# A transposition of attention weights issued one step later in a two-feed-forward kernel

## The chip, the cores and the metric

The kernel runs on one core of a Trainium2 chip. The metric is the device time of one execution in microseconds (us), the median of several runs. A core has five engines that this text speaks of: TensorE (PE, matrix products; PEld is its loading of weights), VectorE (DVE), ScalarE (ACT), GpSimd (POOL) and SyncE (SP, which here issues the DMA transfers). Each works through its own queue in order; they wait for each other by semaphores. Products go to a memory of their own, PSUM, from which VectorE and ScalarE read them.

## The reference

12480 tokens of 128 features go through an attention over 32 inducing rows and back, then through two feed-forward layers of width 2048.

```python
def mab(q, kv):
    s = scale * (q @ kv.transpose(0, 2, 1))
    s = s - s.max(-1, keepdims=True)
    a = np.exp(s)
    a /= a.sum(-1, keepdims=True) + 1e-09
    return a @ kv
h = mab(I, x)                 # 32 inducing rows over all tokens
x = mab(x, h)                 # all tokens over the 32 rows
h = x @ w_in                  # first feed-forward
x = (h * np.clip(h + 3.0, 0.0, 6.0) / 6.0) @ w_out
r = np.maximum(x @ w2_in, 0.0)   # second feed-forward
return (r * r) @ w2_out
```

## The kernel before

The first pass (up to some 40 us) makes the 32 rows `h`. The second pass takes the tokens in 26 chunks of 480 (`CH`), each of four blocks of 120 (`BLK`). All is kept with the features on the partitions and the tokens along the row.

A chunk takes NP = 8 steps, numbered p = 0 to 7; k counts the steps of all chunks, c the chunks. In a step the kernel does two of the sixteen slices of 128 of both feed-forwards, the second one OFF = 11 steps behind the first, so with tokens of an earlier chunk. In each step of the repeating part TensorE runs, in this order:

- `up1`: two products into `h1` (line 567), from the chunk's attention weights `at`. The matrix product of attention with `h` and the first w_in are folded into one 128-row matrix `m4`; so `at` of a chunk is needed from its first step on.
- `up2`: six products into `h2` (line 643), from the first feed-forward's output in an upper and a lower part, `yh` and `yl`.
- in some steps, a part of the next chunk's attention.
- `down1` and `down2`: six products each into the accumulators `yacc` and `oacc` (line 614; in the first steps in plain float32, line 602), from steps L1 = 2 and L2 = 3 back.

That makes 20 products of 480 columns a step. Between them ScalarE and VectorE gate `h1` (`gate1`: a ReLU on ScalarE, line 574, then a product on VectorE, line 575), split the result into an upper part (`hi`, GpSimd, line 586) and a lower part (`lo`, VectorE, line 594), and do likewise for `h2` on ScalarE (lines 653, 657, 667) and VectorE (`lo`, line 673).

The next chunk's attention is spread over the steps of the current chunk: the scores at p = 1 (`att_scores`, tile `ps`), maximum and exponential at p = 2 (`att_exp`, tile `pst`), the norm at p = 4 (`att_norm`: on VectorE a sum, a reciprocal, a product, a cast and two subtractions, the last on line 540; on ScalarE a cast, line 538; the result is `a4`, shown as `a` in a profile), and the turn (`att_turn`). The turn lays the weights of 480 tokens, which lie with the tokens on the partitions, the other way round: four products with a unit matrix into the PSUM tile `pt` (line 550), and a copy on ScalarE from `pt` into `at` (line 555).

`h1`, `h2`, `ps`, `pst` and `pt` take turns in three PSUM buffers (`hp`, tag "h"): each new tile waits until the tile three before it has been read. The accumulators have buffers of their own.

What sets the order: in the first pass, and from step KM = 24 on (at 145 us or so), the order of the engines' queues is that of the code. For the steps before KM, in which the feed-forwards' weights, which come as float64, are also converted (lines 174 to 242, by a plan of ticks, on VectorE, ScalarE and GpSimd), a scheduler sets the order from the code's order and its own estimates. SyncE's order is the code's throughout.

Of the kernel before, what the change touches and what calls it, by code (L numbers as in the profile page):

```python
# [18 lines left out]
SP = mybir.EngineType.SP  # L19

P = 128
BLK = 120          # tokens of a block: one partition each
CH = 480           # tokens of a chunk: four blocks
EPS = 1e-09
CW = 512           # columns of a weight that are converted at a time

# groups of the first pass: tokens of the blocks of each of the four token runs
GROUPS = [(128,) * 2] + [(128,) * 4] * 4 + [(128, 128, 48), (128,) * 2, (128,) * 2]
KEPT = 5           # the group of the last tokens: it stays on chip for the first chunks
TURN_V = {}       # quarters of a group's turned blocks that VectorE copies, ScalarE the others  # L30
NATURAL = {7}      # groups that are loaded in both layouts
# loads of the first pass: groups of tokens (x, and n in the other layout), quarters of the first
# feed-forward's w_in (a) and w_out (b)
LOADS = [("x", 0), ("x", 1), ("x", 2), ("a", 0), ("x", 3), ("x", 4), ("a", 1), ("a", 3), ("a", 2),
         ("x", 5), ("b", 3), ("x", 6), ("b", 0), ("x", 7), ("n", 7), ("b", 2), ("b", 1)]
# for each quarter of the weights (a, b, and c, d for the second feed-forward): the ticks at which its
# conversion starts and at which it is cut in two (two ticks a group of the first pass, PRE up to the
# second pass, then two a step), the engines of the steps (v, p, s: VectorE, GpSimd, ScalarE), and
# whether the sign takes a product of its own
PLAN = {  # L40
    ("a", 0): (4, None, "--v", False),
    ("a", 1): (6, None, "--v", False),
# [12 lines left out]
    ("d", 2): (53, 62, "ssvpv", False),  # L55
    ("d", 3): (58, 62, "--vpv", False),
}
# steps whose parts go to another engine than the rest's
HIGH1_S = {0, 1, 3, 4, 6, 7, 9, 13, 14, 18, 19, 20, 22, 23}   # ScalarE instead of GpSimd
LOW1_P = {1, 2, 4, 5, 6, 7, 8, 11}    # GpSimd instead of VectorE  # L60
HIGH2_P = {0, 1, 6, 7, 10, 12}        # GpSimd instead of ScalarE
LOW2_P = {}  # GpSimd instead of VectorE
N1 = 13            # steps of the first w_out that go in float32 as it is
OFF = 11           # steps from a first product of one feed-forward to the other's
L1, L2 = 2, 3      # steps from a first product to the second
MIX = (0, 3)       # steps of the third and fourth quarter of the mixed weights
PRE = 26           # ticks before the second pass
KM = 24            # steps up to which the engines' order is the scheduler's
RA, RB = 4, 4      # quarters of the first w_in, of the other weights that are on chip as float64
WB = 8             # quarters that are there in float32  # L70
TAIL = 8           # last steps whose upper parts GpSimd makes
LAST = 2           # chunks that stay on chip from the first pass


@with_exitstack
def induced_attention_then_two_ffn(
# [44 lines left out]
    ep = ctx.enter_context(tc.tile_pool(name="ep", bufs=3))  # L121
    sp = ctx.enter_context(tc.tile_pool(name="sp", bufs=2))

    # the last groups of the first pass are the first chunks of the second: they are still on chip
    order = list(range(NCH - LAST, NCH)) + list(range(NCH - LAST))
    x_of = {}

# [3 lines left out]
        nc.sync.dma_start(t, xT[:, n:n + CH])  # L131
        x_of[c] = t

    # A float64 weight comes as two words. Its absolute value is rounded to float32 as
    # (2^20 + v) * power of two, v being the fraction's upper 20 bits with the lower word behind
    # the point; the sign is put on last. What is far below float32's range of use (2^-106) becomes
    # zero. Where an upper and a lower part are asked for, the two add up to the float32 exactly.
    engine_of = {"v": nc.vector, "p": nc.gpsimd, "s": nc.scalar}
    src_of = {"a": w1a, "b": w1b, "c": w2a, "d": w2b}

# [17 lines left out]

    whole, parts, raws, held = {}, {}, {}, []

    # the first feed-forward's w_in in float32 lies where the upper parts of its w_out come to lie
    def float_of(item):
        kind, q = item
        if kind == "a":
# [85 lines left out]
    live, ticks = [], []  # L250
# [22 lines left out]

    waiting = [(kind, q) for kind in "bcd" for q in range(4) if (kind, q) not in LOADS]

# [1 line left out]
    NKEEP = run[KEPT] * J  # L277
    assert LAST * CH <= NKEEP
    t0 = [sum(run[i] for i in range(g) if i != KEPT) * J for g in range(NG)]
# [3 lines left out]
    first = ExitStack()  # L283
    first.enter_context(tc.manual_schedule())
    with ExitStack() as pro:
        pp = pro.enter_context(tc.tile_pool(name="pp", bufs=1))
        pps = pro.enter_context(tc.tile_pool(name="pps", bufs=1, space=PSUM))

        # the tensor engine's clock comes up before the first tokens are there
        fill(18, pps, "xt", 4)  # L290

        nc.sync.dma_start(ind, indT)
# [94 lines left out]
                    )  # L387
            nc.scalar.copy(hsb[:, g, :], acc)

        # the groups' softmaxes brought to their common maximum  # L390
        def common_max():
            nmin = pp.tile([P, 1], F32, name="nmin")
            nc.vector.tensor_reduce(out=nmin, in_=nmax, axis=AX.X, op=ALU.min)
# [45 lines left out]
        rw, rl = weigh(nm4)  # L439
        accumulate(NG - 1)  # L440
        tick()
        # all groups but the last by their weights, four times below each other, and together
        pg = pps.tile([P, D], F32, tag="xt", name="pg", bufs=4)
        for g in range(NG - 1):
            j = g % J
# [20 lines left out]
        )  # L466
        tick()

# [1 line left out]
    hp = ctx.enter_context(tc.tile_pool(name="hp", bufs=3, space=PSUM))  # L470
    ap_ = ctx.enter_context(tc.tile_pool(name="accp", bufs=1, space=PSUM))
    wpool2 = ctx.enter_context(tc.tile_pool(name="wpool2", bufs=1))
# [3 lines left out]
        o = order[c] * CH - (NT - NKEEP)  # L476
        x_of[c] = xlast[:, o:o + CH]

    # inducing rows times w_in: the first feed-forward's weights on 32 rows, four times below
    # each other, as upper, upper, lower and lower parts  # L480
    mixed = {}

    def mix(q):
# [15 lines left out]
    def att_scores(c):  # L499
        ps = hp.tile([P, BLK], F32, tag="h", name="ps")  # L500
        for b in range(J):
            nc.tensor.matmul(  # L502
                ps[M * b:M * (b + 1), :], lhsT=ht4[:, 0, :], rhs=x_of[c][:, b * BLK:(b + 1) * BLK],
                start=True, stop=True,
            )
        s = sp.tile([P, BLK], F32, tag="s", name="s")
        nc.scalar.mul(s, ps, SCALE)
        att[c] = s

    def att_exp(c):  # L510
        s = att.pop(c)
        pt = hp.tile([BLK, J, M], F32, tag="h", name="pst")
        nc.tensor.transpose(pt.rearrange("p j i -> p (j i)"), s, ident)
# [128 lines left out]
            for n, (w, y) in enumerate(((wh, yh[c]), (wl, yh[c]), (wh, yl[c]))):  # L642
                nc.tensor.matmul(h2[k][:, u, :CH], lhsT=w, rhs=y, start=(n == 0), stop=(n == 2))  # L643

    # the last step goes in halves
    def sides(k):
        return (slice(0, 1), slice(1, 2)) if k == K - 1 else (slice(0, 2),)

# [68 lines left out]
    behind = ExitStack()  # L717
# [5 lines left out]
    for k in range(K + OFF + L2 + 1):  # L723
        if k == KM:
            behind.close()
            ctx.enter_context(tc.manual_schedule())
        c, p = divmod(k, NP)
        j = k - OFF
        on(up1, k)
        on(low1, k - 1)  # L730
        tick()
        on(gate1, k)
        on(high1, k)
        on(square2, j - 1)
        on(up2, j)
        on(relu2, j)
        on(high2, j - 1)
        on(low2, j - 2)
        tick()
        if k in MIX:  # L740
            q = MIX.index(k) + 2
            mix(q)
            mix_high(q)
            mix_low(q)
        if c + 1 < NCH:
            if p == 0 and LAST < c + 2 < NCH:
                load_x(c + 2)
            if p == 1:
                att_scores(c + 1)
            if p == 2:  # L750
                att_exp(c + 1)
            if p == 4:
                att_norm(c + 1)
            if p == 5:
                att_turn(c + 1)
        on(down1, k - L1)
        on(down2, j - L2)
# [28 lines left out]
```

## Time and profile before

| | us |
|---|---|
| median of 3 runs | 1013.14 |
| lowest and highest run | 1013.09, 1014.53 |
| span of the profiled execution | 1011.0 |
| TensorE busy | 985.3 |
| ScalarE busy | 845.3 |
| VectorE busy | 833.5 |
| GpSimd busy | 389.6 |

The span runs from the first to the last instruction of one profiled execution; it is 2.1 us below the median of the timed runs, which hold what lies around it as well. The page's parts are: the busy time of the engines, the chain of work that ended last (followed back from the last instruction to what released each), and the costliest groups. Apart from the page, a trace can be asked for waits (who waited for whom, in total, and how often) and for the timeline of an engine: start, duration, instruction and, in brackets, how long the engine was idle before it and what ended that. The durations of neighbouring products overlap, as they are pipelined; the distance between their starts is what a product costs in a row of them.

### The profile page before, as it was taken

To read this page: it belongs to the slowest core of one execution; us is meant where nothing else is said; L and a number is where in the kernel's file an instruction comes from. 1 tells how busy PE (TensorE), PEld (TensorE's weight loads), DVE (VectorE), ACT (ScalarE), POOL (GpSimd) and SP (SyncE) were. 2 spreads that over 40 slices of the span, in tenths; PEclk is the share of its full clock that TensorE was granted. 3 is DMA by queue.
4 is the path that set the end of the run, shared out by engine and by line. 5 is a ranking of instruction groups with operands and counts; after the bars stand their busy time and mean duration, and the time that the engine had idled before them with its cause. 6 is when DMAs were issued, how large, how long until landed. Compare 5 with 4: busy or idle time off the path is not lost.

```text
span 1011.0 us, 12988 instructions
## 1 busy us (share of the span) xinstructions
PE 985.3 (97%) x4911; PEld 818.1 (81%) x4911; DVE 833.5 (82%) x1012; ACT 845.3 (84%) x1041; POOL 389.6 (39%) x236
## 2 busy tenths in 40 slices
PE   9769999999999999999999999999999999999998
PEld 6436788888888888888888888888888888888887
DVE  5998978888888878888888887888888888788764
ACT  6657888888888888888888888888888888888886
POOL 0374433433334344343333434434333343443423
PEclk9899999999999999999999999999999999999999
DMA  9530000000000000000000000000000000000000
GB/s 343 172 113 10 1 20 20 1 20 21 1 20 20 20 1 20 21 1 20 20 1 20 20 20 1 20 20 0 20 20 1 20 20 19 2 11 10 1 10 20
DMA packets 15118, 28.44 MB, mean 28 GB/s; under 512 B 1360, under 2 KB 13008, under 8 KB 14544
## 3 DMA queue, kind: packets, MB, share of 16 engines
q1 hardware_dynamic: 15056, 27.61, 8.3%
q8 instruction: 39, 0.64, 0.3%
q14 instruction: 23, 0.19, 0.1%
HBM read 21.22 MB, written 6.39 MB: 27 GB/s over the span
## 4 chain that ended last, share of the span: by engine, by line
PE 79%; DVE 15%; ACT 2%; issue 1%; POOL 1%; DMA 1%; SPq 0%; ACTq 0%; POOLq 0%
PE oacc L614 23%; PE yacc L614 22%; PE h L643 21%; PE h L567 7%; DVE g L575 4%; DVE lo L673 2%; ACT g L574 1%; DVE lo L594 1%; PE pt L550 1%; POOL hi L586 1%; DVE le L529 1%; DVE a L540 1%; PE ps L502 1%; DMA raw<-in_w1a 1%; DVE cva L179 1%
## 5 line engine op out<-in xcount | busy, mean ns | idle before, releaser
L586 POOL TENSOR_SCALAR hi<-g 128x960 fp32r<-128x960 f32 x188 | 331.6, 1764 | 527.3 <-DVE g L575 527.3
L594 DVE TENSOR_TENSOR lo<-g,hi 128x960 fp32r<-128x960 f32 x195 | 226.9, 1163 | 95.7 <-POOL hi L586 93.2
L574 ACT ACTIVATE g<-h,three 128x960 f32<-128x960 f32 x208 | 220.7, 1062 | 91.8 <-PE h L567 91.7
L673 DVE TENSOR_TENSOR lo<-g,hi 128x960 fp32r<-128x960 f32 (+1 forms) x209 | 240.3, 1150 | 11.8 <-POOL hi L662 7.1
L575 DVE SCALAR_TENSOR_TENSOR g<-g,h 128x960 f32<-128x960 f32 x208 | 239.0, 1150 | 11.0 <-ACT g L574 7.7
L657 ACT ACTIVATE g<-g 128x960 f32<-128x960 f32 (+1 forms) x209 | 207.4, 993 | 0.3
L653 ACT ACTIVATE g<-h 128x960 f32<-128x960 f32 (+1 forms) x209 | 200.4, 960 | 6.1 <-PE h L643 6.1
L667 ACT CAST hi<-g 128x960 fp32r<-128x960 f32 x196 | 193.5, 988 | 0.0
L643 PE MATMUL h<-yh,wh 128*128 128x480 f32 x416 | 158.1, 380 | 0.0
L643 PE MATMUL h<-yh,wl 128*128 128x480 f32 x416 | 157.4, 378 | 0.0
L643 PE MATMUL h<-yl,wh 128*128 128x480 f32 x416 | 157.1, 378 | 0.0
L567 PE MATMUL h<-at,m 128*128 128x480 f32 x416 | 128.3, 390 | 0.6 <-ACT at L555 0.6
L614 PE MATMUL oacc<-hi,wh 128*128 128x480 f32 x416 | 124.9, 381 | 0.0
L614 PE MATMUL oacc<-lo,wh 128*128 128x480 f32 x416 | 124.1, 379 | 0.0
L614 PE MATMUL oacc<-hi,wl 128*128 128x480 f32 x416 | 123.2, 377 | 0.0
L614 PE MATMUL yacc<-hi,wh 128*128 128x480 f32 x390 | 121.6, 392 | 1.4 <-DVE yl L632 1.4
L614 PE MATMUL yacc<-hi,wl 128*128 128x480 f32 x390 | 115.9, 378 | 0.0
L614 PE MATMUL yacc<-lo,wh 128*128 128x480 f32 x390 | 115.9, 378 | 0.0
L567 PEld LDWEIGHTS h<-at,m 128*128 128x128 f32 x416 | 78.4, 190 | 18.3 <-issue 4.0
L643 PEld LDWEIGHTS h<-yh,wh 128*128 128x128 f32 x416 | 78.0, 188 | 13.1 <-ACT g L653 0.4
L614 PEld LDWEIGHTS oacc<-hi,wl 128*128 128x128 f32 x416 | 78.2, 188 | 12.5
L614 PEld LDWEIGHTS oacc<-hi,wh 128*128 128x128 f32 x416 | 77.9, 187 | 12.6 <-issue 0.4
(118 smaller groups left out, 947.1 us busy)
## 6 DMA issues: line engine op xcount, KB each, us to landing
outT<-osb SPq DMA_DIRECT2D x25, 240.0 KB, 2.0
xc<-in_xT SPq DMA_DIRECT2D x24, 240.0 KB, 2.6
xg<-in_xT SPq DMA_DIRECT2D x4, 1024.0 KB, 7.4
raw<-in_w1a SPq DMA_DIRECT2D x4, 512.0 KB, 8.8
raw<-in_w1b SPq DMA_DIRECT2D x4, 512.0 KB, 9.1
raw<-in_w2a SPq DMA_DIRECT2D x4, 512.0 KB, 3.8
raw<-in_w2b SPq DMA_DIRECT2D x4, 512.0 KB, 3.8
xg<-in_xT SPq DMA_DIRECT2D x3, 512.0 KB, 10.2
```

The source lines that it names most:

```text
L179: nc.vector.tensor_scalar(out=a, in0=high, scalar1=0xFFFFF, scalar2=0x100000, op0=ALU.bitwise_and, op1=ALU.bitwise_or,)
L567: nc.tensor.matmul(h1[k][:, u, :CH], lhsT=m4[:, f * P:(f + 1) * P], rhs=a_t[c], start=True, stop=True)
L574: nc.scalar.activation(g1[k], h, AF.Relu, bias=three)
L575: nc.vector.scalar_tensor_tensor(out=g1[k], in0=g1[k], scalar=6.0, in1=h, op0=ALU.min, op1=ALU.mult)
L586: nc.gpsimd.tensor_scalar(out=hi1[k], in0=g1[k], scalar1=1.0, scalar2=1.0, op0=ALU.mult, op1=ALU.mult)
L594: (nc.gpsimd if k in LOW1_P else nc.vector).tensor_tensor(out=lo1[k], in0=g1.pop(k), in1=hi1[k], op=ALU.subtract)
L614: nc.tensor.matmul(acc, lhsT=w[:, f * P:(f + 1) * P], rhs=g[:, u, :], start=(p == 0 and n == 0), stop=(p == NP - 1 and n == 5),)
L643: nc.tensor.matmul(h2[k][:, u, :CH], lhsT=w, rhs=y, start=(n == 0), stop=(n == 2))
L653: nc.scalar.activation(g2[k][:, u, :], h[:, u, :CH], AF.Relu)
L657: nc.scalar.activation(g2[k][:, u, :], g2[k][:, u, :], AF.Square)
L667: nc.scalar.copy(hi2[k][:, u, :], g2[k][:, u, :])
L673: (nc.gpsimd if k in LOW2_P else nc.vector).tensor_tensor(out=lo2[k][:, u, :], in0=g[:, u, :], in1=hi2[k][:, u, :], op=ALU.subtract)
```

## The change

`att_turn` of the next chunk is called at the end of the step p = 6 in place of p = 5. All else in the diff takes away comments and spaces.

```diff
             if p == 4:
                 att_norm(c + 1)
-            if p == 5:
+            if p == 6:
                 att_turn(c + 1)
         on(down1, k - L1)
```

In the built program this moves rows on TensorE and ScalarE in each chunk from KM on. TensorE in the middle of the run, before: the turn (`pt`) stands between `up2` of p = 5 (`h_3061`) and the `down` products of that step; `h_3096` is `up1` of p = 6.

```order
L643 MATMUL h_3061<-yl,wh 128x480
L550 MATMUL pt<-ident_r,a_3033 128x120 x4
L614 MATMUL yacc<-hi_2973,wh 128x480 x2
L614 MATMUL yacc<-hi_2973,wl 128x480 x2
L614 MATMUL yacc<-lo_3023,wh 128x480 x2
```

TensorE at the same place after; `h_3089` and `h_3100` are `up1` and `up2` of p = 6, and `hi_3009` belongs to `down1` of that step.

```order
L567 MATMUL h_3089<-at,m_78 128x480 x2
L643 MATMUL h_3100<-yh,wh 128x480
L643 MATMUL h_3100<-yh,wl 128x480
L643 MATMUL h_3100<-yl,wh 128x480
L643 MATMUL h_3100<-yh,wh 128x480
L643 MATMUL h_3100<-yh,wl 128x480
L643 MATMUL h_3100<-yl,wh 128x480
L550 MATMUL pt<-ident_r,a_3033 128x120 x4
L614 MATMUL yacc<-hi_3009,wh 128x480 x2
```

The turn now stands one whole step of TensorE later. ScalarE around the same turn, as a difference (`h_3096` of before is `h_3089` of after, and so on):

```order
 L667 CAST hi_3070<-g_3019 128x960
-L555 CAST at<-pt 128x480
-L574 ACTIVATE g_3101<-h_3096,three 128x960
+L574 ACTIVATE g_3094<-h_3089,three 128x960
 L657 ACTIVATE g_3068<-g_3068 128x960
-L653 ACTIVATE g_3114<-h_3107 128x960
-L667 CAST hi_3116<-g_3068 128x960
+L653 ACTIVATE g_3107<-h_3100 128x960
+L667 CAST hi_3109<-g_3068 128x960
+L555 CAST at<-pt 128x480
 L574 ACTIVATE g_3138<-h_3133,three 128x960
```

The copy out of `pt` has gone behind four instructions of the step p = 6. In the steps before KM the scheduler orders anew. VectorE there, in the first chunk of the second pass, before, from the conversions ahead of three gates (line 575) to the first `yl`:

```order
L205 TENSOR_SCALAR w_868<-raw 128x512
L189 SCALAR_TENSOR_TENSOR cva<-raw,cva 128x512
L174 TENSOR_SCALAR cve<-raw 128x512
L179 TENSOR_SCALAR cva<-raw 128x512
L240 CAST wh<-w_709 128x512
L575 SCALAR_TENSOR_TENSOR g_861<-g_861,h_852 128x960
L575 SCALAR_TENSOR_TENSOR g_876<-g_876,h_872 128x960
L575 SCALAR_TENSOR_TENSOR g_887<-g_887,h_884 128x960
L189 SCALAR_TENSOR_TENSOR cva<-raw,cva 128x512
L205 TENSOR_SCALAR w_982<-raw 128x512
L174 TENSOR_SCALAR cve<-raw 128x512
L575 SCALAR_TENSOR_TENSOR g_897<-g_897,h_894 128x960
```

VectorE at the same place after (`g_854` is `g_861` of before):

```order
L575 SCALAR_TENSOR_TENSOR g_854<-g_854,h_845 128x960
L189 SCALAR_TENSOR_TENSOR cva<-raw,cva 128x512
L205 TENSOR_SCALAR w_861<-raw 128x512
L575 SCALAR_TENSOR_TENSOR g_876<-g_876,h_872 128x960
L575 SCALAR_TENSOR_TENSOR g_887<-g_887,h_884 128x960
L174 TENSOR_SCALAR cve<-raw 128x512
L179 TENSOR_SCALAR cva<-raw 128x512
L575 SCALAR_TENSOR_TENSOR g_897<-g_897,h_894 128x960
L632 SCALAR_TENSOR_TENSOR yl<-yacc,yh 128x480
L515 TENSOR_REDUCE nm<-pst 120x4
L240 CAST wh<-w_709 128x512
```

The gates have moved ahead of conversions, and the cast `wh<-w_709` and a set of conversions (`w_982`) behind `yl`.

## Rows read from the trace of the kernel before

**Rows 1.** The page, parts 1 and 4: busy time, and the chain's shares.
```profile
PE 985.3 (97%) x4911; PEld 818.1 (81%) x4911; DVE 833.5 (82%) x1012; ACT 845.3 (84%) x1041; POOL 389.6 (39%) x236
...
PE 79%; DVE 15%; ACT 2%; issue 1%; POOL 1%; DMA 1%; SPq 0%; ACTq 0%; POOLq 0%
```

**Rows 2.** Waits from 140 us on: waiter, awaited, us, times, longest.
```profile
PEld pt L550 <- ACT a L538: 12.2, 22, 1.0
```

**Rows 3.** TensorE's timeline, mid run: start, duration, instruction, count, idle before.
```profile
597.90 0.59 PE L567 MATMUL h<-at,m 128*128 128x480 f32 x2
...
599.40 0.38 PE L643 MATMUL h<-yl,wh 128*128 128x480 f32 x1
599.93 0.63 PE L550 MATMUL pt<-ident_r,a 120*128 120x120 f32 x4
...
603.07 0.60 PE L567 MATMUL h<-at,m 128*128 128x480 f32 x2
...
607.39 0.59 PE L567 MATMUL h<-at,m 128*128 128x480 f32 x2
```

**Rows 4.** TensorE's timeline: an unwaited turn's step, then the first and last waiting ones.
```profile
127.71 0.59 PE L567 MATMUL h<-at,m 128*128 128x480 f32 x2
...
129.21 0.38 PE L643 MATMUL h<-yl,wh 128*128 128x480 f32 x1
129.43 0.55 PE L550 MATMUL pt<-ident_r,a 120*128 120x120 f32 x4
...
132.46 0.59 PE L567 MATMUL h<-at,m 128*128 128x480 f32 x2
...
163.84 0.59 PE L567 MATMUL h<-at,m 128*128 128x480 f32 x2
...
169.50 0.59 PE L567 MATMUL h<-at,m 128*128 128x480 f32 x2
...
923.03 0.59 PE L567 MATMUL h<-at,m 128*128 128x480 f32 x2
...
928.23 0.59 PE L567 MATMUL h<-at,m 128*128 128x480 f32 x2
```

**Rows 5.** VectorE's timeline, mid run, around the turn of rows 3.
```profile
599.29 0.49 DVE L540 TENSOR_TENSOR a<-a,a 120x128 fp32r<-120x128 f32 x2
...
600.77 1.15 DVE L575 SCALAR_TENSOR_TENSOR g<-g,h 128x960 f32<-128x960 f32 x1
...
603.27 0.66 DVE L686 COPY osb<-oacc 128x480 f32<-128x480 f32 x1 [0.28 <-PE oacc L614]
...
604.96 1.15 DVE L575 SCALAR_TENSOR_TENSOR g<-g,h 128x960 f32<-128x960 f32 x1
```

**Rows 6.** ScalarE's timeline, mid run, at the same turn.
```profile
602.82 0.57 ACT L555 CAST at<-pt 128x480 fp32r<-128x480 f32 x1
603.76 1.06 ACT L574 ACTIVATE g<-h,three 128x960 f32<-128x960 f32 x1 [0.38 <-PE h L567]
```

**Rows 7.** VectorE's timeline in the steps before KM.
```profile
43.78 0.42 DVE L179 TENSOR_SCALAR cva<-raw 128x512 uint32<-128x512 uint32 x1
...
45.39 1.50 DVE L179 TENSOR_SCALAR cva<-raw 128x512 uint32<-128x512 uint32 x1
...
72.20 3.27 DVE L575 SCALAR_TENSOR_TENSOR g<-g,h 128x960 f32<-128x960 f32 x3
...
78.95 1.15 DVE L575 SCALAR_TENSOR_TENSOR g<-g,h 128x960 f32<-128x960 f32 x1 [2.21 <-ACT g L574]
...
81.04 0.66 DVE L632 SCALAR_TENSOR_TENSOR yl<-yacc,yh 128x480 fp32r<-128x480 f32 x1 [0.60 <-ACT yh L631]
...
115.32 0.64 DVE L632 SCALAR_TENSOR_TENSOR yl<-yacc,yh 128x480 fp32r<-128x480 f32 x1
```

**Rows 8.** TensorE's timeline in the steps before KM.
```profile
73.48 3.54 PE L602 MATMUL yacc<-g,w 128*128 128x480 f32 x4 [5.20 <-DVE g L575]
...
116.11 0.67 PE L614 MATMUL yacc<-hi,wh 128*128 128x480 f32 x2 [1.36 <-DVE yl L632]
```

## Prediction

> **What bounds the kernel now.** I read the page first. TensorE is busy in 97% of the span and carries 79% of the chain that ended last [rows 1], so only time that TensorE loses can be won back. Then the list of waits, from 140 us on, where all the weights are converted and the chunks repeat: the one wait of TensorE's weight loads that belongs to the moved step is the load for `pt` (line 550), 12.2 us in 22 times [rows 2]. It waits for the attention weights `a`, which VectorE and ScalarE make in `att_norm`. Third, TensorE's timeline around such a turn. I count a chunk's steps by p, from 0 to 7; a step of TensorE runs from its first product with `at` (line 567) to the next step's. In the middle of the run the step with the turn (p = 5) lasts 603.07 - 597.90 = 5.17 us, and the next one, which holds nothing but its 20 products, 607.39 - 603.07 = 4.32, or 0.216 a product [rows 3]. The last product ahead of the turn starts at 599.40, so the turn could start 0.216 later, at 599.62; it starts at 599.93. VectorE shows why: its last instruction for `a` (line 540) starts at 599.29, takes 0.49 and so ends at 599.78, 0.15 ahead of the turn [rows 5]. TensorE runs in order and stands still there once a chunk.
>
> What a turn costs that does not wait is in the trace too. In the chunk before the repeating ones the scheduler happens to have the weights ready in time: the turn starts 129.43 - 129.21 = 0.22 behind the product ahead of it, and its whole step lasts 132.46 - 127.71 = 4.75 us [rows 4].
>
> **The change part by part.** *The turns that wait.* No instruction is added or removed. Four small products on TensorE and one copy on ScalarE (`at`, line 555) move from the end of step p = 5 to the end of step p = 6; the DMA queue and GpSimd's order in the repeating chunks stay. With the turn one step of 4.32 us later the weights are there some four microseconds early, so the step p = 5 becomes a plain one of 4.32 and the step p = 6 one with an unwaited turn, 4.75. Before, the two are 5.17 + 4.32 = 9.49; after, 9.07. There are 22 such turns behind 140 us: the first lasts 169.50 - 163.84 = 5.66, which is 0.91 above 4.75; the other 21 alternate between some 5.17 and 5.20, and the last is 928.23 - 923.03 = 5.20 [rows 4]. Their mean of 5.185 is 0.435 above 4.75. The sum is 0.91 + 21 x 0.435 = **10.0 us**. The lower bound takes only the distance between starts as gain, 0.53 - 0.22 = 0.31 for a usual turn: 0.91 - 0.12 + 21 x 0.31 = 7.3.
>
> The four products of a turn each load fresh weights, and the step with an unwaited turn is 4.75 - 4.32 = 0.43 longer than a plain one [rows 3, 4]. The Trainium skill (TensorE: Matmul & The Clock Gate, section LDWEIGHTS) has a weight load last its columns over 1.2 GHz, for four loads of 128 columns 0.43 us; the same page's section Back-to-back issue gap has a lone product take N/2.4 + 2.5 ns, for four of 120 columns 0.21. By the first the sum is the 10.0 above; by the second each turn would win 0.22 more, 4.8 in all. The trace agrees with the first.
>
> *What is late next.* Without its wait TensorE reaches step p = 6 earlier by 0.85 (the wait, and the turn itself, which is gone from p = 5), at 597.90 + 4.32 = 602.22 on the old clock, and that step's second first product (`up2`) 0.43 later, at 602.65. The three PSUM buffers of tag "h" go round, and with `pt` no longer between them, `up2` of p = 6 takes the buffer of `h1` of p = 5, which VectorE's gate (line 575) must have read. VectorE is behind in just that step, since the norm lies in it; the gate starts at 600.77 and ends at 601.92 [rows 5]. With the 0.15 of above that is 602.07, **0.58 us early**. So no wait, with little to spare. Behind the moved turn the first product of p = 7 takes the buffer of `h1` of p = 6: it comes at 602.22 + 4.75 = 606.97, and the gate of p = 6, which VectorE's order holds behind `lo` of p = 5, ends at 604.96 + 1.15 = 606.11: 0.7 early [rows 5]. The copy of the old output accumulator (603.27, line 686) lies before that and rather comes sooner, since its products do.
>
> *The copy `at`.* It moves on ScalarE behind four instructions of the next step. From the start of the turn to the end of `at` it takes 602.82 + 0.57 - 599.93 = 3.46 us [rows 3, 6]. From the moved turn to the next chunk's first product there are 0.43 of the turn, 12 products of 0.216 and one step: 0.43 + 2.59 + 4.32 = 7.34. It is 3.9 early and costs nothing; its cover is that whole seventh step.
>
> *The head.* For the steps up to KM the scheduler sets the order, and it orders anew: VectorE no longer has five conversions in a row ahead of three gates at 72.20, but the first gate ahead of most of them, and it puts several conversions behind `yl`. Where it stands now, VectorE is full up to its second `yl` at 115.32, but for 2.21 us ahead of 78.95 and 0.60 ahead of 81.04 [rows 7], and TensorE waits 1.36 for that `yl` [rows 8]. The later end of this stretch can come forward by what VectorE idles, 2.21 + 0.60 = 2.8. The other bound above: TensorE's own wait at 73.48, 5.20 us [rows 8], all gone. Below, the conversions that are put off may run into others: nothing, or a loss. I take 2.0, near the 2.8, since `yl` itself moves ahead in the order.
>
> The profiled span is 1011.0, 2.1 below the median of 1013.1, as launch and end lie outside it; the change touches neither. **1013.1 - 10.0 - 2.0 = 1001.1 us.**
>
> **The rivals.** *The conversions collide.* On VectorE the same instruction of line 179 lasts 0.42 us in one place and 1.50 in another, 1.08 more, where GpSimd works beside it [rows 7]. The new order of the head puts conversions beside other GpSimd work; four more such meetings cost 4.3, and the head turns from -2.0 to +2.3: 1013.1 - 10.0 + 2.3 = 1005.4. For it: some ten instructions of VectorE change places there. Against: those moved were stretched themselves before. The Trainium skill (SBUF — State Buffer, Who interferes with whom) says that VectorE and GpSimd share a port pair under an exclusive lock, the loser blocked for the other's whole instruction; the two durations agree with that.
>
> *The ring takes the place of the wait.* If VectorE's gate of p = 5 came 1.0 us later than worked out, `up2` would wait 0.42 and every turn's gain would be gone: 1013.1 - 2.0 = 1011.1. For it: the margin of 0.58 is the smallest of all. Against: the gate hangs on VectorE's own queue, which does not move, and not on the turn.
>
> *The wait is for something else.* If the turn now waited for its PSUM buffer and not for `a`, it would wait one step later too; 1011.1 again. Against: the 0.15 us between VectorE's end and the turn's start, and the one turn without a wait [rows 4, 5].
>
> *Slower: `at` comes too late.* ScalarE has the moved copy behind a full step's work. If it ran one step (4.32) later than I place it, the next chunk's first product would wait 3.46 + 4.32 + 0.15 - 7.34 = 0.6 us, 22 times 13.2: 1013.1 + 13.2 - 10.0 = 1016.3. It bites from 3.9 us of lateness on, and costs more than the change wins from 4.3. Against: ScalarE is through with its step ahead of the next product, and idles 0.38 us for it right behind the copy [rows 6]; no row has it a step behind.
>
> **How the numbers follow.** Forecast 76%, collisions 10%, the ring 6%, another cause of the wait 4%, slower 4%. The forecast's own spread: 5.20 instead of 2.0 in the head gives 997.9; the small gain of 7.3 with nothing in the head gives 1005.8. The collisions, 1005.4, lie within. So the range is 998 to 1006, which leaves out the last three rivals and some tails. Within 0.2% (2.0 us, about what a measurement of this kernel can tell) are half the ring's and the other cause's cases, 0.07; slower 0.04; faster 0.89.
>
> **What would show it.** Right: steps p = 5 of 4.32 us and p = 6 of 4.75; each chunk some 0.43 shorter than before; no load for `pt` in the waits behind 140 us; the turn of the last chunk some 12 us earlier. The head's part is seen in the start of the first waiting chunk's step, 163.84 before, some 2 earlier after. Wrong: a new wait at line 643 for VectorE's gate (the ring), at line 567 for `at` (slower), more instructions of 1.5 us on VectorE ahead of 115 us (collisions), or a turn that still waits.

## The result and the profile after

The changed kernel takes **1002.13 us** in the median of four runs (1000.44 to 1003.29); the kernel before, beside it on the same chip, takes 1013.79 (four runs, 1013.09 to 1014.53). The ratio is 0.9883, with an interval of [0.9869, 0.9897], so 11.7 us less, between 10.4 and 13.3. In a second comparison of five rounds (below, `a0_after_again`) it is 0.9891 [0.9876, 0.9907].

The profiled execution of the changed kernel is its slowest run (1003.29, span 1001.5), so its trace shows 9.5 us of the gain (1011.0 - 1001.5) and not all 11.7. Its page, parts 1 and 4, against [rows 1]:

```profile
PE 979.4 (98%) x4911; PEld 819.9 (82%) x4911; DVE 829.9 (83%) x1012; ACT 844.5 (84%) x1041; POOL 388.5 (39%) x236
...
PE 90%; DVE 6%; DMA 2%; issue 1%; ACT 0%; POOL 0%; SPq 0%; ACTq 0%; POOLq 0%
```

The same work is done, and TensorE's share of the chain that ended last has grown from 79% to 90%, while VectorE's has fallen from 15% to 6%, as one would expect where the chain no longer leaves TensorE for `att_norm` at each turn.

The waits from 140 us on, against [rows 2] (waiter, awaited, us, times, longest): of TensorE's weight loads this is now the first of the list, and there is no row for `pt` any more. The row itself is not new, the kernel before has it with the same numbers.

```profile
PEld ps L502 <- ACT g L574: 7.3, 22, 0.3
```

TensorE around the same turn in the middle of the run, against [rows 3] (start, duration, instruction, count, idle before): the first products of p = 5, 6 and 7, `up2` of p = 6 with its first and last product, the turn, and the product behind it.

```profile
592.73 0.59 PE L567 MATMUL h<-at,m 128*128 128x480 f32 x2
...
597.04 0.59 PE L567 MATMUL h<-at,m 128*128 128x480 f32 x2
597.47 0.38 PE L643 MATMUL h<-yh,wh 128*128 128x480 f32 x1
...
598.55 0.38 PE L643 MATMUL h<-yl,wh 128*128 128x480 f32 x1
598.77 0.56 PE L550 MATMUL pt<-ident_r,a 120*128 120x120 f32 x4
599.16 0.65 PE L614 MATMUL yacc<-hi,wh 128*128 128x480 f32 x2
...
601.83 0.60 PE L567 MATMUL h<-at,m 128*128 128x480 f32 x2
```

The step p = 5 lasts 597.04 - 592.73 = 4.31 us, the step p = 6 lasts 601.83 - 597.04 = 4.79, and the turn starts 598.77 - 598.55 = 0.22 behind the product ahead of it: it does not wait. VectorE and ScalarE around it, against [rows 5] and [rows 6]:

```profile
594.13 0.49 DVE L540 TENSOR_TENSOR a<-a,a 120x128 fp32r<-120x128 f32 x2
...
595.61 1.15 DVE L575 SCALAR_TENSOR_TENSOR g<-g,h 128x960 f32<-128x960 f32 x1
...
599.79 1.15 DVE L575 SCALAR_TENSOR_TENSOR g<-g,h 128x960 f32<-128x960 f32 x1
...
601.32 0.56 ACT L555 CAST at<-pt 128x480 fp32r<-128x480 f32 x1
602.46 1.06 ACT L574 ACTIVATE g<-h,three 128x960 f32<-128x960 f32 x1 [0.58 <-PE h L567]
```

The weights are done at 594.13 + 0.49 = 594.62, 4.15 us ahead of the turn that reads them. VectorE's gate of p = 5 ends at 596.76 and `up2` of p = 6 starts at 597.47; `at` is ready at 601.88, and its first reader is the step that begins at 601.83 + 4.33 = 606.16.

**Where the 9.5 us of the two traces lie.** I cut both traces at starts of first products (line 567), of which there is one pair a step.

| stretch | before | after | difference |
|---|---|---|---|
| up to the first step of the second pass | 43.88 | 45.01 | +1.13 |
| from there to step KM | 97.39 | 96.94 | -0.45 |
| from KM to the step p = 5 of the first late turn | 22.57 | 22.34 | -0.23 |
| from there to the last chunk's last step (178 steps, 22 turns), called the **steady part** below | 803.33 | 793.43 | **-9.90** |
| from there to the end | 43.8 | 43.8 | 0.0 |

In the steady part the mean step p = 5 goes from 5.205 to 4.310 us, p = 6 from 4.326 to 4.779, and all others stay within 0.01. The first row is not the change's: nothing moves in the first pass.

### The profile page after: what moved, and what is told of

It is laid out like the page before. It is cut to its first block, busy times and chain, and to the rows that moved or that the text cites. A ratio compares the mean times of both kernels' runs of the same rounds, so it can differ in the third digit from the quotient of the medians.

```text
span 1001.5 us, 12966 instructions
## 1 busy us (share of the span) xinstructions
PE 979.4 (98%) x4911; PEld 819.9 (82%) x4911; DVE 829.9 (83%) x1012; ACT 844.5 (84%) x1041; POOL 388.5 (39%) x236
## 4 chain that ended last, share of the span: by engine, by line
PE 90%; DVE 6%; DMA 2%; issue 1%; ACT 0%; POOL 0%; SPq 0%; ACTq 0%; POOLq 0%
PE oacc L614 26%; PE h L643 26%; PE yacc L614 25%; PE h L567 8%; DVE g L575 1%; DMA raw<-in_w1a 1%; PE pt L550 1%; PE ps L502 1%; PE yacc L602 1%; DVE lo L673 1%; DVE cve L174 1%; DMA xg<-in_xT 1%; DVE lo L594 1%; PE xt L359 0%; DVE cva L189 0%
## 5 line engine op out<-in xcount | busy, mean ns | idle before, releaser
L673 DVE TENSOR_TENSOR lo<-g,hi 128x960 fp32r<-128x960 f32 (+1 forms) x209 | 241.5, 1156 | 11.7 <-POOL hi L662 6.8
L643 PEld LDWEIGHTS h<-yl,wh 128*128 128x128 f32 x416 | 78.0, 188 | 12.2
```

Source lines behind the costliest of these rows:

```text
L673: (nc.gpsimd if k in LOW2_P else nc.vector).tensor_tensor(out=lo2[k][:, u, :], in0=g[:, u, :], in1=hi2[k][:, u, :], op=ALU.subtract)
```

## The experiments

The theory: the turn waited for the attention weights, one step gives VectorE the time, and nothing else becomes late. Rivals: the wait would have come back at the PSUM buffers (the ring), it was for something else, the copy `at` becomes late, or the gain is that of the head (the steps before KM, which the scheduler ordered anew). All kernels compute the whole result. "Steady" is the steady part of the run's trace; the last column is the gain of the medians less the gain in the steady part, so what the rest of the program brought.

| run | median (runs) | before beside it | ratio | steady | p = 5, 6, 7 | rest |
|---|---|---|---|---|---|---|
| before | 1013.79 (4) | | | 803.33 | 5.205, 4.326, 4.320 | |
| after | 1002.13 (4) | 1013.79 | 0.9883 [0.9869, 0.9897] | 793.43 | 4.310, 4.779, 4.328 | 1.8 |
| `a0_after_again` | 1002.59 (4) | 1013.01 | 0.9891 [0.9876, 0.9907] | 793.44 | 4.310, 4.780, 4.327 | 0.5 |
| `e1_late_turn` | 1004.40 (4) | 1013.01 | 0.9911 [0.9898, 0.9925] | 793.46 | 4.310, 4.780, 4.328 | -1.3 |
| `e2_head_turn` | 1011.65 (11) | 1013.01 | 0.9984 [0.9975, 0.9992] | 802.78 | 5.181, 4.330, 4.317 | 0.8 |
| `e3_norm3_turn5` | 1005.03 (4) | 1013.01 | 0.9917 [0.9903, 0.9930] | 794.09 | 4.782, 4.327, 4.321 | -1.3 |
| `e4_turn7` | 1007.32 (4) | 1013.67 | 0.9934 [0.9919, 0.9949] | 797.85 | 4.310, 4.318, 4.842 | 0.9 |
| `e5_norm5_turn6` | 1011.83 (10) | 1013.67 | 0.9982 [0.9972, 0.9991] | 801.55 | 4.311, 5.137, 4.330 | 0.1 |
| `e6_late_pad2` | 1009.16 (4) | 1013.67 | 0.9956 [0.9939, 0.9972] | 799.45 | 4.314, 4.773, 4.577 | 0.6 |
| `e7_early_pad2` | 1013.99 (10) | 1013.67 | 1.0003 [0.9994, 1.0013] | 803.38 | 5.212, 4.326, 4.320 | -0.3 |
| `e8_ring` | 1003.36 (4) | 1013.28 | 0.9910 [0.9893, 0.9926] | 793.43 | 4.310, 4.780, 4.327 | 0.0 |
| `e9_ring_pad2` | 1020.68 (4) | 1013.28 | 1.0074 [1.0059, 1.0089] | 810.37 | 4.313, 5.522, 4.329 | -0.4 |
| `e10_ring_pad_half` | 1002.46 (4) | 1013.28 | 0.9903 [0.9883, 0.9923] | 793.61 | 4.311, 4.772, 4.327 | 1.1 |

### The two parts of the change apart

`a0_after_again` is the changed kernel itself. `e1_late_turn` moves the turn only where the order is the code's, so the head keeps the order of before; `e2_head_turn` moves it only in the head.

Against the changed kernel, `e1_late_turn`:

```diff
             if p == 4:
                 att_norm(c + 1)
-            if p == 6:
+            if p == (6 if k >= KM else 5):
                 att_turn(c + 1)
```

And `e2_head_turn`:

```diff
             if p == 4:
                 att_norm(c + 1)
-            if p == 6:
+            if p == (5 if k >= KM else 6):
                 att_turn(c + 1)
```

> The changed kernel once more, beside the three that follow, to see how far its head varies. Theory (the turns' wait is the whole gain that lasts): the stretch from the first late turn's step to the last first product of a chunk lasts 793.4 us as in its first trace, 9.9 less than before; the time lies 8.5 to 13 us below the kernel before, and what varies lies ahead of 45 us or in the scheduler's steps. Rival (the head itself wins 2.0 as predicted): the head up to the first late turn's step, counted from the first product of the second pass, is 2.0 shorter in the trace again, not 0.7.

> The turn at p = 6 only from step KM on; in the scheduler's steps it stays at p = 5, so the head's order is that of before. Theory: 9.9 us less than before (about 1003.5), from steps of 4.32 and 4.78 in place of 5.18 and 4.32. Rival (the new order of the head is worth 2.0): 1.5 to 2.5 slower than the changed kernel beside it; theory: within 1 of it.

> The turn at p = 6 only before step KM, at p = 5 from there on. Theory: 0 to 1 us less than before, with the 5.20 us wait of the head gone and new waits in its place. Rival as predicted: 2.0 less. Either: the 21 late turns' steps still last 5.18.

`e1_late_turn` has the whole steady gain (793.46) and 8.6 of the 10.4 us that the changed kernel gains beside it. That is 1.8 us slower than the changed kernel, outside of the 1 us that I had expected and inside the range of the rival (a head worth 2.0); the intervals of the two ratios, some 1.5 us either way each, leave it open. `e2_head_turn` keeps the wait, as its list of waits from 140 us on says:

```profile
PEld pt L550 <- ACT a L538: 11.8, 22, 0.6
```

It gains 1.4 us (0.8 to 2.5 by the interval of the ratio), between the 0 to 1 that I had expected and the rival's 2.0. So the repeating chunks carry the gain, and the head some 1 to 2 us. Of the latter 0.55 lies in the steady part (803.33 - 802.78), most of it in the first late turn, whose step lasts 5.66 with the old head [rows 4] and no more than 5.20 with the new one.

### Which distance counts

If the turn waited for the weights, it is the distance from norm to turn that matters, not the place of the turn. `e3_norm3_turn5` leaves the turn at p = 5 and makes the norm one step earlier, `e5_norm5_turn6` moves both one step later.

Against the changed kernel, `e3_norm3_turn5`:

```diff
-            if p == 4:
+            if p == (3 if k >= KM else 4):
                 att_norm(c + 1)
-            if p == 6:
+            if p == 5:
                 att_turn(c + 1)
```

And `e5_norm5_turn6`:

```diff
-            if p == 4:
+            if p == (5 if k >= KM else 4):
                 att_norm(c + 1)
-            if p == 6:
+            if p == (6 if k >= KM else 5):
                 att_turn(c + 1)
```

> The turn stays at p = 5, but from step KM on the norm that makes its weights comes one step earlier, at p = 3. Theory (the turn waits for the weights): the wait goes here too, p = 5 lasts 4.75 to 4.80, and the time is 9 to 10 less than before, as with the later turn. Rival (the turn waits for a PSUM buffer or for its place in the queue): steps of 5.18 as before and the time of before.

> From step KM on both the norm and the turn one step later than before, at p = 5 and p = 6, so one step apart as before. Theory (the distance from norm to turn decides): the wait is back, a step of 5.15 to 5.3 at p = 6, and the time is that of before within 2. Rival (the place p = 6 is what helps): p = 6 stays at 4.78 and 9.9 are won.

`e3_norm3_turn5`: the turn stands where it stood before, its step lasts 4.782, and the steady part is 794.09. `e5_norm5_turn6`: the turn stands where the change puts it, and it waits again. Its last product of `up2` ahead of the turn, and the turn, on TensorE:

```profile
603.47 0.38 PE L643 MATMUL h<-yl,wh 128*128 128x480 f32 x1
603.95 0.63 PE L550 MATMUL pt<-ident_r,a 120*128 120x120 f32 x4
```

VectorE's last instruction for the weights:

```profile
603.31 0.50 DVE L540 TENSOR_TENSOR a<-a,a 120x128 fp32r<-120x128 f32 x2
```

And the turn's row in the waits from 140 us on:

```profile
PEld pt L550 <- issue: 10.1, 21, 0.5
```

The turn starts 0.48 behind the product ahead of it in place of 0.22, and its step is 0.36 longer than an unwaited one. The profile names no releaser here ("issue"), but VectorE's line does: the weights are done at 603.31 + 0.50 = 603.81, 0.14 ahead of the turn, as before (0.15). And the pair of runs says the same: with the norm a step ahead of the turn, wherever they stand, TensorE waits; with two steps between, it does not. The wait was for the weights. `e5_norm5_turn6` is still 1.8 us better in the steady part than before; 1.5 of that lies in the turn's own step (5.137 in place of 5.205, 22 times), and why I did not follow up.

### Can the turn go later still

`e4_turn7`, against the changed kernel:

```diff
-            if p == 6:
+            if p == (7 if k >= KM else 5):
                 att_turn(c + 1)
```

> From step KM on the turn at p = 7, one step later still. By the working of the prediction (3.46 us from the turn's start to the end of the copy, 0.15 on top, 3.02 until the next chunk's first product) that product waits 0.6 at the copy, 22 times 13: about 3 slower than before. By the trace of the changed kernel, where the chain from turn to copy is 3.11, it waits 0.2, 22 times 4 to 5: 5 less than before. Rival (a later turn is always as good, the copy hides): no wait at line 567, 9.9 less than before.

Now `at` has 12 products left until its first reader. The timelines of TensorE (the step p = 7, its turn, and the next chunk's first two steps) and of ScalarE (the copy):

```profile
603.90 0.59 PE L567 MATMUL h<-at,m 128*128 128x480 f32 x2
...
605.63 0.55 PE L550 MATMUL pt<-ident_r,a 120*128 120x120 f32 x4
...
608.75 0.71 PE L567 MATMUL h<-at,m 128*128 128x480 f32 x2
...
613.18 0.59 PE L567 MATMUL h<-at,m 128*128 128x480 f32 x2
...
608.12 0.57 ACT L555 CAST at<-pt 128x480 fp32r<-128x480 f32 x1
```

And the wait from 140 us on:

```profile
PEld h L567 <- ACT at L555: 6.6, 22, 0.3
```

The copy ends at 608.69 and the next chunk's first product starts right behind it, at 608.75. From turn to the end of `at` it takes 608.69 - 605.63 = 3.06 us. The wait costs some 0.2 us a turn, over half of it in the next chunk's first step (4.45 in place of 4.33) and most of the rest in the step p = 7 (4.842), 4.4 us in the steady part. So, while the norm is at p = 4, p = 6 is the one of the three places tried that has no wait: a step earlier the turn waits, a step later it is waited for.

### How near the next wait is

By the prediction the gate of p = 5 on VectorE is the next thing to be late, by a margin of 0.58. To see it I put VectorE behind by a known time: two additions on a scratch tile of 128x480, which nobody reads, ahead of that gate. `e6_late_pad2` has them in `e1_late_turn`, `e7_early_pad2` in the kernel before.

```diff
+        if k >= KM and p == 5 and c + 1 < NCH:
+            for _ in range(2):
+                nc.vector.tensor_tensor(out=pad, in0=pad, in1=pad, op=ALU.add)
         on(gate1, k)
```

> As with the late turn from step KM on, and VectorE adds a scratch tile of 480 columns to itself twice ahead of its gate of p = 5, some 1.2 us more. Theory (the three PSUM buffers leave the gate 0.56 us of margin): the second product group of p = 6, line 643, waits 0.5 to 0.7 for that gate, 22 times 11 to 15, so the kernel lands at the time of before or up to 5 above it. Rival (the gate has ample time): 9.9 less than before, no wait at line 643.

> The kernel before with the same two scratch additions ahead of the gate of p = 5. Theory (with the turn at p = 5 the ring leaves that gate 1.4 us): nothing waits for it, the time is that of before within 2. Rival (VectorE is so full that any work there costs): 22 times 1.2 more, some 20 to 26 us slower than before.

In `e7_early_pad2` the 1.26 us cost nothing (803.38 in place of 803.33); why, is taken up below. In `e6_late_pad2` they cost 6.0 us, some half of what I had expected, and not in the step p = 6, which keeps its 4.773, but in p = 7. The gate of p = 5 and that of p = 6 on VectorE, then on TensorE `up2` of p = 6, the first product of p = 7 and `up2` of p = 7 (line numbers are 2 higher here):

```profile
636.05 1.15 DVE L577 SCALAR_TENSOR_TENSOR g<-g,h 128x960 f32<-128x960 f32 x1
...
640.23 1.15 DVE L577 SCALAR_TENSOR_TENSOR g<-g,h 128x960 f32<-128x960 f32 x1
...
636.52 0.38 PE L645 MATMUL h<-yh,wh 128*128 128x480 f32 x1
...
640.86 0.59 PE L569 MATMUL h<-at,m 128*128 128x480 f32 x2
641.43 0.48 PE L645 MATMUL h<-yh,wh 128*128 128x480 f32 x1
```

`up2` of p = 6 starts at 636.52 while the gate of p = 5 runs until 637.20. It cannot be writing the buffer which that gate reads. The semaphores in the built program say the same: in the changed kernel `up2` of p = 6 waits for VectorE, `pt` for ScalarE, `up1` of p = 7 for VectorE and `up2` of p = 7 for ScalarE; in `e6_late_pad2` it is ScalarE, VectorE, ScalarE, VectorE. The pool does not hand out its three buffers in turn as a rule. With the pad in the code it handed out others, and it was the gate of p = 6, which the pad had also put back, that `up2` of p = 7 waited for. My experiment had changed two things.

So had `e7_early_pad2`. Its gate of p = 5 on VectorE, then on TensorE the first product of p = 6 and `up2`:

```profile
601.87 1.15 DVE L577 SCALAR_TENSOR_TENSOR g<-g,h 128x960 f32<-128x960 f32 x1
...
602.91 0.60 PE L569 MATMUL h<-at,m 128*128 128x480 f32 x2
603.35 0.38 PE L645 MATMUL h<-yh,wh 128*128 128x480 f32 x1
```

In the kernel before, the first product of p = 6 waits for VectorE and `up2` for ScalarE; here it is the other way round. The gate ends at 603.02, after that product has begun and 0.33 ahead of `up2`. With the buffers of before, that product would have had to wait, by my estimate some 0.2 us a turn. So the run shows that the pad is free with these buffers, and not that the kernel before had 1.26 us to spare.

`e8_ring`, `e9_ring_pad2` and `e10_ring_pad_half` take the choice away: three tags with one buffer each, and a counter. The first is the changed kernel with that alone, the second has the same pad, the third one addition of 240 columns.

```diff
-    hp = ctx.enter_context(tc.tile_pool(name="hp", bufs=3, space=PSUM))
+    hp_pool = ctx.enter_context(tc.tile_pool(name="hp", bufs=1, space=PSUM))
+    class Ring:
+        n = 0
+        def tile(self, shape, dtype, tag, name, bufs=None):
+            self.n += 1
+            return hp_pool.tile(shape, dtype, tag=tag + str(self.n % 3), name=name, bufs=1)
+    hp = Ring()
```

> The changed kernel, with the three PSUM buffers of tag h handed out strictly in turn (three tags of one buffer each and a counter) in place of the pool's own choice. From the first late turn on the built program has after's order and waits; the head's order differs a little, since the scheduler chose otherwise there. Control for the two padded kernels beside it. Theory (margins of a strict ring): from the first late turn to the last step 793.4 us, step p = 6 4.78, no wait. Rival (the pool's choice hides a wait): a wait at up2 of p = 6 or up1 of p = 7 and more than 793.4.

> The strict ring with the same two scratch additions of 480 columns on VectorE ahead of the gate of p = 5 as in the earlier padded kernel, 1.27 us together. In that earlier kernel the pool had handed out the buffers otherwise: the built program let up2 of p = 6 wait for ScalarE, pt for the gate of p = 5 and up2 of p = 7 for the gate of p = 6. Here up2 of p = 6 has to wait for the gate of p = 5 again. Theory (the margin there is 0.56): up2 of p = 6 waits 1.27 - 0.56 = 0.7 a turn, 21 to 22 times, some 15 us; step p = 6 5.5, from the first late turn to the last step 808 or so, slower than with the pool's own choice (799.4) by some 9. Rival (VectorE isn't bound to that place, or the margin is larger by what TensorE's later arrival gives): 793.4 to 799.5.

> The strict ring with one scratch addition of 240 columns on VectorE ahead of the gate of p = 5, some 0.35 us by the 480-column ones. Theory (margin 0.56): no wait, 793.4 us from the first late turn to the last step, step p = 6 4.78, same time as the strict ring without it. Rival (there is no margin, up2 of p = 6 already starts when the gate lets it): 0.35 a turn, 7.5 us.

`e8_ring` has the steady part of the changed kernel to the hundredth, 793.43: there the pool had gone in turn by itself. In `e9_ring_pad2` the wait comes where it was expected. Pad and gate of p = 5 on VectorE, then the first products of p = 6 and of p = 7 on TensorE:

```profile
605.80 1.34 DVE L745 TENSOR_TENSOR pad<-pad 128x480 f32<-128x480 f32 x2
607.06 1.14 DVE L586 SCALAR_TENSOR_TENSOR g<-g,h 128x960 f32<-128x960 f32 x1
...
607.24 0.59 PE L578 MATMUL h<-at,m 128*128 128x480 f32 x2
608.26 0.48 PE L654 MATMUL h<-yh,wh 128*128 128x480 f32 x1 [0.42 <-DVE g L586]
...
612.71 0.60 PE L578 MATMUL h<-at,m 128*128 128x480 f32 x2
```

And the waits from 140 us on:

```profile
PEld h L654 <- DVE g L586: 19.0, 22, 1.1
PE h L654 <- DVE g L586: 10.1, 22, 0.7
```

The gate ends at 608.20 and `up2` starts at 608.26 in place of 607.67. The pad takes 607.06 - 605.80 = 1.26 us of VectorE and delays `up2` by 0.59, so 0.67 of it was free here; over all turns the step p = 6 grows by 5.522 - 4.780 = 0.74, by which 0.52 were free. In the steady part that is 16.9 us, and the kernel is **0.7% slower than before**, 1.0074 [1.0059, 1.0089]. `e10_ring_pad_half` delays the gate by 0.31 (this is its gate behind the pad, and `up2` of p = 6, which starts 0.43 behind its step as ever):

```profile
594.12 0.40 DVE L745 TENSOR_TENSOR pad<-pad 128x240 f32<-128x240 f32 x1
594.43 1.15 DVE L586 SCALAR_TENSOR_TENSOR g<-g,h 128x960 f32<-128x960 f32 x1
...
595.55 0.59 PE L578 MATMUL h<-at,m 128*128 128x480 f32 x2
595.98 0.38 PE L654 MATMUL h<-yh,wh 128*128 128x480 f32 x1
```

It costs 0.2 us in all 178 steps together. The margin is real: more than 0.31, and by `e9_ring_pad2` 0.5 to 0.7 us.

## Why the prediction was right, point by point

**What bounds the kernel: right.** The one wait of [rows 2] was the gain, and no other engine took its place.

**The waiting turns: 10.0 us expected, 9.90 measured.** The price of a turn that does not wait came from a single one, in the chunk ahead of the repeating ones (4.75, [rows 4]); the 22 moved ones have a mean of 4.779. The plain step was taken as 4.32 and is 4.310. Per chunk that leaves 9.09 for the two steps in place of 9.07. The lower bound of 7.3, which counted only the distance between starts, was too careful: the step shortened by more than the visible gap, since the waiting turn of [rows 3] lasted 0.63 where it now lasts 0.56, and the product behind it came 0.47 after its start where it now comes 0.39 after. A step with an unwaited turn is 0.46 longer than a plain one (4.779 - 4.32). That is near the 0.43 estimated from the Trainium skill's rule for a weight load (TensorE: Matmul & The Clock Gate, section LDWEIGHTS), and far from the 0.21 that the prediction estimated from the same page's section Back-to-back issue gap; the steps of all 22 moved turns, 4.77 to 4.79, agree with the first.

**What is late next: right in place and size.** Expected 0.58 of margin at `up2` of p = 6; in the trace after, 597.47 - 596.76 = 0.71 from the gate's end, 0.56 with the 0.15 that the prediction took for the handing over, and two pads bracket it. For the first product of p = 7 the 0.7 expected are 601.83 - 600.94 - 0.15 = 0.74. The step of the argument that held by luck is the rule behind it, that the three buffers go round: it is true of this program and was not of the two padded ones without the strict ring.

**The ring as a rival (6%)** did not come, but its mechanism is there: `e9_ring_pad2` is that rival made by hand. Its condition was put as 1.0 us of lateness for all of the gain to go. In `e9_ring_pad2` 1.26 us cost 0.74 a turn, and the gain is 0.45 a turn; with 0.3 less, at just under 1.0, the two would be equal by this estimate.

**The wait for something else (4%): refuted** by `e3_norm3_turn5` and `e5_norm5_turn6`.

**The copy `at`: right that it costs nothing, its chain was mis-sized.** The 3.46 us from turn to `at`, taken from [rows 3, 6], is 601.88 - 598.77 = 3.11 after the change and 3.06 in `e4_turn7`: in the kernel before, the long turn itself and the later products stood in it. So the margin is 4.3 and not 3.9; and a turn at p = 7, which by 3.46 would wait 3.46 + 0.15 - 3.02 = 0.6, waits 0.2. The slower rival (4%) would have needed ScalarE a whole step behind; it ends the copy at 601.88 and then stands idle for 0.58 until the next product is there for it.

**The head: the one term that the runs do not confirm in size.** Expected were 2.0 us, with 5.20 above and a loss below. The big wait at 73.48 [rows 8] is gone, as the new order of the gates let hope: TensorE's step of 80.70 before starts at 77.09 now. But it is given back at other places. The step before, then TensorE's larger waits after from that step on, then VectorE and GpSimd ahead of the largest:

```profile
80.70 0.68 PE L567 MATMUL h<-at,m 128*128 128x480 f32 x2
```

```profile
77.09 0.71 PE L567 MATMUL h<-at,m 128*128 128x480 f32 x2 [0.70 <-DVE g L575]
...
96.36 0.71 PE L567 MATMUL h<-at,m 128*128 128x480 f32 x2 [0.90 <-DVE g L575]
...
107.25 1.17 PE L614 MATMUL oacc<-hi,wl 128*128 128x480 f32 x2 [2.49 <-POOL wl L242]
...
118.25 0.67 PE L614 MATMUL yacc<-hi,wh 128*128 128x480 f32 x2 [0.58 <-DVE yl L632]
...
97.77 1.15 DVE L594 TENSOR_TENSOR lo<-g,hi 128x960 fp32r<-128x960 f32 x1
...
103.82 2.24 DVE L594 TENSOR_TENSOR lo<-g,hi 128x960 fp32r<-128x960 f32 x1 [0.89 <-POOL hi L586]
...
103.76 3.43 POOL L242 TENSOR_TENSOR wl<-w,wh 128x512 fp32r<-128x512 f32 x2
```

Counted from the first step of the second pass, 36.82 before and 32.08 after, 4.7 us were won up to that step and 4.3 lost behind it, so 0.45 remain. The two conversions `wl` of line 242 that GpSimd now does at 103.76 are its sixth and seventh in the second pass; before, the sixth and the seventh stand at two places, and TensorE waits for neither:

```profile
82.54 1.30 POOL L242 TENSOR_TENSOR wl<-w,wh 128x512 fp32r<-128x512 f32 x1 [3.33 <-ACT wh L238]
...
99.32 4.66 POOL L242 TENSOR_TENSOR wl<-w,wh 128x512 fp32r<-128x512 f32 x1 [0.51 <-ACT wh L238]
```

So what the new order puts off has a reader on TensorE. This is the step that the prediction left out: it took VectorE's idle time and TensorE's wait at 73.48 for what could be won, and did not ask which product needs the conversions that were put off.

Instructions are also stretched at that place: VectorE's `lo` beside the two `wl` takes 2.24 us, where the same subtraction at 97.77 takes 1.15. Stretching of this kind is what the rival "the conversions collide" (10%) is about; the Trainium skill (SBUF — State Buffer, Who interferes with whom) says the two engines lock each other out of a shared port, and the doubled duration agrees. But there is hardly more of it than before. In the stretch from the first step of the second pass to KM, VectorE has 15 instructions before and 16 after that last over 0.3 us longer than the shortest of their line and shape, 12.9 and 13.7 us longer in all; GpSimd has 11 and 10, with 10.4 and 9.7 us. So that rival, which needed four more such meetings, did not come. How the lost 4.3 us divide between the later order and the stretched instructions there is not shown.

How much it is on average the runs don't settle well. In the traces with the old order of the head (before, `e1_late_turn`, `e3_norm3_turn5`, `e4_turn7`, `e5_norm5_turn6`, and `e6_late_pad2` and `e7_early_pad2`, which have one memset more) the stretch to KM lasts 96.07 to 100.03 us; with the new one (after, `a0_after_again`, `e2_head_turn`) 96.94, 97.46 and 96.96. Executions of one order differ there by more than the change brings. By the last column of the table the three kernels with the new order gain 1.8, 0.5 and 0.8 beyond the steady part, the six with the old one -1.3, -1.3, 0.9, 0.1, 0.6 and -0.3: 1.2 between the means, with a scatter of about 1. From the first step of the second pass to the first late turn's step the traces need 119.96 before, 119.28 after and 119.80 in `a0_after_again`, so 0.7 and 0.2 less. The sign was right, and 2.0 looks rather high, though the interval of `e2_head_turn` does not exclude it; with the 9.9 of the steady part, 1.2 make 11.1 of the 11.7 measured.

**Two of the signs named at the end were wrongly derived.** The turn of the last chunk was to come some 12 us earlier; but the turn itself moves a step back, and it comes 5.06 earlier (925.09 before, 920.03 after), the chunk's step p = 5 9.0 earlier. And the first late step was to start some 2 earlier than 163.84; it starts at 164.29 in the trace, since its first pass took 1.13 longer and the head won 0.7 and not 2.0. The sign of collisions, more instructions of 1.5 us on VectorE, did not appear.

## What to carry to other kernels

Where an engine that runs in order stands still for a result that another engine makes a little too late, issue the consumer one step later and count what is left on both sides: here the producer then had 4.15 us to spare, the next reader 4.3, and one more step cost nearly half of the gain. The time that is won brings the busy engine earlier to its other hand-overs, so the smallest margin there decides: 0.56 us here, and 1.26 us more work on VectorE in that step turned the change into a loss. Before pricing a wait on buffers that go round, read in the built program which instruction each one waits for, and read it again for every experiment.

## What the runs showed that I had not expected

- **A pad changes more than a delay.** The same 1.26 us of extra work on VectorE cost 6.0 us where the pool chose the buffers, and 16.9 where they went strictly in turn, with not one product different.
- **The head differs from one execution to the next.** Up to the first step of the second pass the traces need 42.9 to 46.1 us, and from there to KM, with one and the same order, 96.96 to 100.03 (five of them), while the 178 steady steps of the four traces with the same order there (after, `a0_after_again`, `e1_late_turn`, `e8_ring`) agree within 0.03 us (793.43 to 793.46). A change to such a head wants many timed runs; a change to the steady part is read from one trace. What makes the head differ is not shown.
- **TensorE's clock is part of the head, too.** In the trace before, its granted clock is 0.50 from 72.0 to 78.7 us, around the wait of 5.20 at 73.48. In two traces of the changed kernel, after and `a0_after_again`, TensorE stands still for `wl` (2.49 and 2.48 us), and right behind it their clocks differ. The same stretch in both, where the third number from the end is the granted clock:

```profile
107.20:110.40 3.20, 3.15 (x8) 2.67 (x9) 3.20 (x4) 0.68 (x2) 0.44 (x1) 0.50 0.00 0
...
107.20:110.40 3.20, 2.52 (x12) 1.86 (x12) 3.20 (x5) 1.89 (x2) 0.78 (x1) 1.00 0.00 0
```

In the first it is at the lower of its two levels (1.2 and 2.4 GHz), and eight products take 110.57 - 107.25 = 3.32 us from start to start, 1.6 more than at 0.216 each. In the second it stays at the upper level, but TensorE then waits 0.68 for VectorE's gate. Counted from the first step of the second pass, the step with the wait for `wl` starts at 55.78 and at 56.32, and the step after the next at 69.57 in both. So by these two traces the lower clock cost some 0.5 us there, and not 1.6.
